# A reciprocal moved ahead of the value products, and one weight piece moved from the gated block into the second pair of heads

## The chip, the cores and the metric

The kernel runs on one core of a Trainium2 chip. The metric is the device time of one execution in microseconds; the times shown are medians of repeated runs. TensorE appears as PE (matmul) and PEld (weight load), VectorE as DVE, ScalarE as ACT, GpSimd as POOL, and SyncE as SP, which here only issues DMAs.

## What is computed

The first half is attention with a hash mask: a query sees only those keys whose six sign bits under a random projection agree with its own. Its output, rearranged to 3072 tokens of 512 channels, goes through a gated feed-forward block.

```python
batch, n_heads, seq, head_dim = (4, 8, 768, 64)
q_bits = (np.einsum('bhsd,dk->bhsk', q, proj) > 0)
mask = q_bucket[:, :, :, None] == k_bucket[:, :, None, :]
scores = np.where(mask, scale * np.matmul(q, k.transpose(0, 1, 3, 2)), -1000000000.0)
attn = np.exp(scores - max) ; attn = attn / (sum(attn) + 1e-09)
attn_out = np.matmul(attn, v)
x = attn_out.transpose(0, 2, 1, 3).reshape(B * S, H * D)      # 3072 x 512
g = x @ w_gate                                                # 512 x 1536
out = (g * sigmoid(g) * (x @ w_val)) @ w_out                  # 1536 x 512
```

The weights of the feed-forward block arrive as 64-bit floats and are read as pairs of 32-bit words.

## The kernel before

**Attention** goes through 16 pairs of heads, n = 0 to 15, four pairs to each of four batches. For each pair, 12 units (two halves of the queries by six blocks of 128 keys) are scored on PE (`score`, L523) into PSUM tiles of two banks; the pool `pp` has four such tiles for everything. ScalarE takes the exponential of each (L533), VectorE adds the exponentials up (`add`), and PE multiplies them with the values (`attend`, L554) into one further PSUM tile, which ScalarE copies to `xT` (L560, L561).

**The row sums** take a detour. `total(n)` adds across partitions on PE (L590); `fetch_row` copies the row (ScalarE, L595) and sends it by a small DMA on SP to a tile `few`, then puts `invert` on the list `waiting`. `settle()` runs what is on that list: `invert` takes the reciprocal on VectorE (L603), writes it to DRAM (`sums`, L605, SP) and reads it back spread over the partitions into `r` (two DMAs, L612, SP); it returns `norm`, which goes on the list `last`. `norm` (L619, VectorE) multiplies `xT` by `r`; for batches after the first it then writes the result to DRAM (L623, SP). In pair n's iteration `settle()` stands near the top and inverts pair n - 2, since `total(n - 1)` is run late in iteration n; after the loop it is called once more, and inverts pair 14. Pair 15's reciprocal is left for the gated block (`left`, L918: after the sixth and the fourteenth step there).

**The weight pieces.** The three weight matrices are cut into 36 pieces. Each piece is loaded (`words`, three buffers), scaled by ScalarE (`scale`, L139 and L140), widened by VectorE (`widths`, L153, L155, L158, after which the load of the piece three places on is issued), rounded by ScalarE (`round_up`, L146), split into parts by VectorE (`parts`, L166 and L168) and written to DRAM (`ram`, L170). Piece i lives in half i % 2 of a tile `stage` that it shares with its neighbour; the pool `stagep` has two such tiles.

In the attention loop this work is spread over the pairs. Near the end of iteration n, `begin_pieces(PACE[n])` first rounds the pieces widened before, then scales PACE[n] new ones, in ScalarE's order ahead of the value copy and of the next pair's exponentials. After the value products `keep_pieces()` takes the parts of all pieces widened so far and writes them to DRAM (POOL issues). The new ones are widened at the top of iteration n + 1. With PACE = 1, 1, 2, 1, 2, 1, ... 23 of the 36 are scaled by the end of the loop. The gated block does the others, one each in `turn()`: seven steps, dealt out between its own operations; there SP issues the DMAs.

**The gated block** goes through three blocks of 1024 tokens. For each of 12 slices of the hidden width (`U`), PE multiplies for the gate and then for the value, each as a group `a` of 16 matmuls and a group `n` of 8 (L711), into one PSUM tile each. ScalarE reads `a` (L750), VectorE subtracts `n` (L756), ScalarE applies the activation (L758), VectorE multiplies (L760) and splits (L767, L770). After each third slice (`D`), eight output chunks of 9 matmuls (`o`, L711) are added into accumulators (L811 or L813, then L817). The weights come back from DRAM through a ring of six tiles (`bring`, L251, POOL): three of the buffers are there from the start, three are allocated with the gated block. The order on each engine is the order of the program text; tiles are handed on by their pools.

Of the kernel before, what the change touches and what calls it, by code (L numbers as in the profile page):

```python
# [19 lines left out]
def kernel(  # L20
# [68 lines left out]
    def finish(todo):  # L89
        while todo:  # L90
            todo.pop(0)()
# [31 lines left out]
    def load_words(count, queue=None):  # L123
        queue = queue or queues[0]
        for i in range(len(words), min(count, NPIECE)):
            words[i] = t = wordp.tile([P, PIECE, 2], I32, tag="words", name="words")
            to = t.rearrange("p f w -> p (f w)")
            if len(pieces[i].shape) == 3:
                to = to.rearrange("p (j c) -> p j c", j=NJ)
            queue.dma_start(to, pieces[i])  # L130

    def scale(i):
        t = words[i]
        if i // 2 not in stages:
            stages[i // 2] = stagep.tile([P, 2, 3, PIECE], FP32, tag="stage", name="stage")
        staged[i] = st = stages[i // 2][:, i % 2]
        top = t.rearrange("p f w -> p (f w)").bitcast(U16)
        top = top.rearrange("p (f w) -> p f w", w=4)[:, :, 1]
        nc.scalar.activation(st[:, 1], t[:, :, 1].bitcast(FP32), AF.Copy, scale=2.0**-112)  # L139
        nc.scalar.activation(t[:, :, 0], top, AF.Copy, scale=2.0**-13 * (1 + 2.0**-17))  # L140
        progress["scaled"] = i + 1

    def round_up(i):
        if i not in rounded:
            st = staged[i]
            nc.scalar.activation(r32(st[:, 0]), st[:, 1], AF.Copy, scale=TOWARD)  # L146
            rounded.add(i)
# [26 lines left out]
    def begin_pieces(count):  # L174
        for i in sorted(added - rounded):
            round_up(i)
        for i in range(progress["scaled"], min(progress["scaled"] + count, NPIECE)):
            load_words(i + 1)
            scale(i)

    def keep_pieces():
        for i in range(progress["kept"], progress["scaled"]):
            if i in added:
                for _ in parts(i):
                    pass

    def widen_pieces():
        for i in range(progress["kept"], progress["scaled"]):
            if i not in added:
                for _ in widths(i):  # L190
                    pass
# [49 lines left out]
    def bring(count=1):  # L241
        for _ in range(count):
            i = len(held)
            if i == len(wanted):
                return
            what, n = wanted[i]
            at = place[what, n % NF]
            assert progress["kept"] > at, (i, at, progress)
            pool = ringp[i % sum(RINGS) >= RINGS[0]]
            held[what, n] = t = pool.tile([P, 3, PIECE], FP32R, tag="ring", name="ring")  # L250
            nc.gpsimd.dma_start(t.bitcast(FP32), ram[at].bitcast(FP32))  # L251
# [53 lines left out]
    def attention(scope):  # L305
# [39 lines left out]
        def load(n, names):  # L345
            if n < len(pairs):
                for name in names:
                    fetch(n, name, nc.sync)
# [187 lines left out]
        def score(u):  # L536
            if u % (2 * NCH):
                products(u)
                mark(u)
            else:  # L540
                banks_of[u] = two_banks("sc")[:, :, 0:HQ]
                product(u, bits, True, False)
                product(u, T, False, True)
                mark(u, False)

        def attend(u):
            n, half, c = units[u]
            a = weights(u)
            if (half, c) == (0, 0):
                av[n] = two_banks("av")  # L550
            ps = av[n][:, half]
            width = AW if half == 0 else HQ
            for h in range(2):
                nc.tensor.matmul(ps[h * D : (h + 1) * D, 0:width], raws["v", n][:, h, c, :],  # L554
                                 a[:, h, 0:width], start=c == 0, stop=c == NCH - 1)
            if (half, c) == (1, NCH - 1):
                pool, tag = (xp, "xT") if n < len(pairs) - 1 else (lastp, "last")
                xT[n] = pool.tile([P, S], FP32, tag=tag, name=tag)
                mean[n] = small.tile([P, 1], FP32, tag="e", name="e")
                nc.scalar.activation(mean[n], av[n][:, 0, HQ : HQ + 1], AF.Copy, scale=EPS)  # L560
                nc.scalar.copy(xT[n].rearrange("p (x q) -> p x q", x=2), av[n][:, :, 0:HQ])  # L561
# [3 lines left out]
        def add(u):  # L565
            n, half, c = units[u]
            if c % 2 == 0:
                return
            first, now = (twos[x % RING // 2][:, :, :, 0:HQ] for x in (u - 2, u))
            if c == 3:  # L570
                t = both[half] = att.tile([P, 2, 2, HQ], FP32, tag="both", name="both", bufs=1)
                nc.vector.scalar_tensor_tensor(out=t, in0=first, scalar=S * EPS / P / 2, in1=now,  # L572
                                               op0=ALU.add, op1=ALU.add)
            elif c > 3:
                t = both[half]
                nc.vector.tensor_tensor(t, t, now, op=ALU.add)  # L576
            if c == NCH - 1:
                acc[n, half] = att.tile([P, 2, HQ], FP32, tag="acc", name="acc", bufs=4)
                nc.vector.tensor_tensor(acc[n, half], t[:, 0], t[:, 1], op=ALU.add)
# [4 lines left out]
        def total(n):  # L584
            ps = joint(n)[:, 0]
            t = [acc.pop((n, half)) for half in range(2)]
            for h in range(2):
                for half in range(2):
                    g = (2 * h + half) * BLOCK
                    nc.tensor.matmul(ps[g : g + BLOCK, 0:HQ], ones, t[half][:, h, :],  # L590
                                     start=True, stop=True)

            def fetch_row():
                row = att.tile([P, HQ], FP32, tag="row", name="row", bufs=1)
                nc.scalar.copy(row, ps[:, 0:HQ])  # L595
                few = small.tile([P, each], FP32, tag="few", name="few")
                nc.sync.dma_start(few, row.rearrange("(g r) t -> r g t", r=BLOCK)[0])
                waiting.append(lambda: invert(n, few))

            return fetch_row  # L600
# [28 lines left out]
        def prepare_pair(count):  # L629
            for _ in range(count):  # L630
                if steps:
                    rest.extend(f for f in steps.pop(0)() or [] if f)

        def settle():
            while waiting:
                last.append(waiting.pop(0)())
# [4 lines left out]
        load_words(3, nc.sync)  # L641
        steps = front(1)
        last = []
        PACE = [1, 1] + [2, 1] * 7
        splits = []
        later = []
        TURN = 5
        for n in range(len(pairs)):
            u = 2 * NCH * n
            more = n + 1 < len(pairs)  # L650
            if n == 1:
                widen_pieces()
            if n and more:
                steps = front(n + 1)
                prepare_pair(2)
            widen_pieces()
            settle()
            for i in range(2 * NCH):
                if u + i > 2:
                    score(u + i)  # L660
                if n == 0 and i == TURN:
                    prepare_pair(2)
                if i % NCH and i < 2 * NCH - 1:
                    add(u + i)
                if i == (2 if n else TURN):
                    load(n + 2, "qk")
            row = total(n - 1) if n else None
            if more:
                prepare_pair(1)
            finish(rest)  # L670
            add(u + 2 * NCH - 1)
            if row:
                row()
            finish(last)
            begin_pieces(PACE[n])
            finish(splits)
            splits.extend(later)
            later.clear()
            for c in range(2 * NCH):
                attend(u + c)  # L680
            load(n + 2, "v")
            keep_pieces()
            if n >= len(pairs) - 3:
                bring()
# [9 lines left out]
    with ExitStack() as scope:  # L694
        attention(scope)
# [264 lines left out]
```

## Time and profile before

| | us |
|---|---|
| median of 3 runs (916.47 to 916.75) | 916.68 |
| the profiled execution | 916.95 |
| its span, first to last instruction | 915.2 |
| attention, until the first matmul of the gated block | 314.5 |
| one pair of heads (PE) | 19.1 |
| one slice `U` of the gated block (PE) | 10.9 |
| eight output chunks `D` (PE) | 16.3 |

The span holds 12450 instructions, and the mean granted TensorE clock is 0.997. VectorE is busiest in the attention stage: 18.5 us of the 19.1 us of pairs 4 to 7, 14.5 in pair 2. ScalarE is at 15 to 17 us per pair. The DMA engines are at a share of 0.45 to 0.98 in the attention stage and at 0.84 between 320 and 376 us, where the ring fills; later they fall to about 0.4.

A line of a timeline gives the start and the duration in us, engine, line, operation, output <- input with shapes, and a count of merged instructions; in brackets the idle time before it and what ended that. A line of the waits gives who waited for whom: us in total, times, the longest. A line of DMA issues gives the count, the size, and the median us from issue to landing.

### The profile page before, as it was taken

How to read it: one execution, taken by the hardware profiler on the slowest of the kernel's cores; microseconds unless marked ns; L12 is line 12 of the kernel's file. 1: busy time of each engine (PE TensorE's matmuls, PEld its weight loads, DVE VectorE, ACT ScalarE, POOL GpSimd, SP SyncE). 2: the span in 40 equal slices, each digit the busy share in tenths (PEclk: the TensorE clock that was granted, in tenths of full speed). 3: DMA queues.
4: the chain of work that ended last, by engine and by line, in shares of the span. 5: the costliest groups of instructions: out<-in, count | busy, mean ns of one | idle time of the engine just before them, and what ended most of it. 6: DMA issues, size and time to landing. Idle time of an engine off the chain costs nothing.

```text
span 915.2 us, 12450 instructions
## 1 busy us (share of the span) xinstructions
PE 904.3 (99%) x4801; PEld 637.2 (70%) x4801; DVE 665.7 (73%) x783; ACT 450.9 (49%) x606; POOL 88.1 (10%) x176
## 2 busy tenths in 40 slices
PE   9999999999999989999999999999999999999998
PEld 4444444444444568788888888888888888888886
DVE  6779999998988748779786955365568754474746
ACT  7688988888787625542523133331313233313220
POOL 1001100011001201000001100101000100001000
PEclk9999999999999999999999999999999999999999
DMA  7576777978796798685867573433444642525232
GB/s 184 103 155 184 185 206 185 219 205 220 216 199 213 239 335 273 236 293 199 322 206 255 179 269 127 173 139 140 148 158 149 244 142 86 219 71 207 103 138 92
DMA packets 143706, 174.24 MB, mean 190 GB/s; under 512 B 103360, under 2 KB 113568, under 8 KB 143648
## 3 DMA queue, kind: packets, MB, share of 16 engines
q0 software_dynamic: 22096, 114.31, 35.6%
q1 hardware_dynamic: 120144, 57.95, 24.7%
q10 hardware_dynamic: 1408, 1.20, 0.5%
q8 instruction: 38, 0.62, 0.3%
q14 instruction: 20, 0.16, 0.1%
HBM read 133.17 MB, written 39.42 MB: 189 GB/s over the span
## 4 chain that ended last, share of the span: by engine, by line
PE 86%; DVE 6%; DMA 3%; ACT 2%; issue 2%; SPq 0%; ACTq 0%; DVEq 0%
PE a L711 24%; PE o L711 19%; PE sc L523 16%; PE av L554 12%; PE n L711 12%; DMA sums<-few 1%; DMA r<-sums 1%; PE joint L590 1%; PE joint L431 1%; DVE v L756 1%; DVE v L760 1%; DVE hid L767 1%; DVE g L756 1%; ACT v L750 1%; DVE stage L158 1%
## 5 line engine op out<-in xcount | busy, mean ns | idle before, releaser
L711 PE MATMUL a<-xparts,ring 128*128 128x512 f32 x1152 | 273.0, 389 | 0.0
L711 PEld LDWEIGHTS a<-xparts,ring 128*128 128x128 f32 x1152 | 216.2, 188 | 45.5 <-issue 0.6
L711 PE MATMUL o<-ring,hid 128*128 128x512 f32 (+1 forms) x870 | 199.3, 389 | 1.5 <-DVE o L817 1.5
L711 PEld LDWEIGHTS o<-ring,hid 128*128 128x128 f32 x870 | 162.6, 188 | 36.5 <-DVE o L817 2.7
L533 ACT ACTIVATE A<-sc 128x768 f32<-128x768 f32 x192 | 153.8, 816 | 0.9
L523 PE MATMUL sc<-qT,kT 64*128 64x384 f32 x768 | 152.8, 483 | 0.2 <-ACT qb L436 0.2
L711 PE MATMUL n<-xparts,ring 128*128 128x512 f32 x576 | 143.8, 392 | 4.3 <-DVE g L756 4.3
L711 PEld LDWEIGHTS n<-xparts,ring 128*128 128x128 f32 x576 | 109.1, 190 | 27.4 <-DVE g L756 4.7
L554 PE MATMUL av<-A,vraw 128*64 128x386 f32 (+1 forms) x768 | 127.7, 488 | 0.0
L756 DVE TENSOR_TENSOR v<-v,n 128x1024 f32<-128x1024 f32 x36 | 44.0, 1221 | 98.0 <-PE n L711 91.8
L251 POOL DMA_DIRECT2D ring<-ram x108 | 57.1, 531 | 506.6 <-PE n L711 330.4
L554 PEld LDWEIGHTS av<-A,vraw 128*64 128x64 f32 x768 | 53.7, 136 | 73.3 <-issue 63.0
L750 ACT ACTIVATE g<-a 128x1024 f32<-128x1024 f32 x36 | 36.9, 1025 | 124.8 <-PE a L711 124.1
L523 PEld LDWEIGHTS sc<-qT,kT 64*128 64x128 f32 x768 | 68.3, 187 | 41.2 <-issue 35.5
L761 ACT ACTIVATE hid<-v 128x1024 fp32r<-128x1024 f32 x36 | 38.2, 1062 | 112.5 <-DVE v L760 112.5
L758 ACT ACTIVATE g<-g 128x1024 f32<-128x1024 f32 x36 | 38.2, 1061 | 97.4 <-DVE g L756 97.4
L817 DVE TENSOR_TENSOR o<-o 128x512 f32<-128x512 f32 x92 | 63.0, 686 | 18.9 <-ACT o L811 16.5
L756 DVE TENSOR_TENSOR g<-g,n 128x1024 f32<-128x1024 f32 x36 | 43.8, 1215 | 31.4 <-PE n L711 31.4
L523 PE MATMUL sc<-qb,kb 64*128 64x384 bf16 x384 | 62.8, 323 | 0.0
L572 DVE SCALAR_TENSOR_TENSOR both<-A 128x1536 f32<-128x1536 f32 x32 | 55.4, 1732 | 6.4 <-ACT A L533 5.0
L767 DVE SCALAR_TENSOR_TENSOR hid<-hid,v 128x1024 fp32r<-128x1024 f32 (+1 forms) x39 | 44.5, 1140 | 19.2 <-ACT hid L761 19.1
L576 DVE TENSOR_TENSOR both<-both,A 128x1536 f32<-128x1536 f32 x32 | 56.0, 1749 | 1.7
(80 smaller groups left out, 691.8 us busy)
## 6 DMA issues: line engine op xcount, KB each, us to landing
ring<-ram POOLq DMA_DIRECT2D x108, 768.0 KB, 5.2
ram<-stage POOLq DMA_DIRECT2D x22, 768.0 KB, 4.6
ram<-stage SPq DMA_DIRECT2D x14, 768.0 KB
vraw<-in_v_dram SPq DMA_DIRECT2D x16, 384.0 KB
out_dram<-o SPq DMA_DIRECT2D x23, 256.0 KB
kraw<-in_k_dram SPq DMA_DIRECT2D x60, 96.0 KB
qraw<-in_q_dram SPq DMA_DIRECT2D x60, 96.0 KB
r<-sums SPq DMA_DIRECT2D x30, 192.0 KB
```

What stands on the lines that cost most here:

```text
L251: nc.gpsimd.dma_start(t.bitcast(FP32), ram[at].bitcast(FP32))
L523: nc.tensor.matmul(banks_of[u][:, h], x["k", n][rows, ks], x["q", n][rows, qs], start=start, stop=stop)
L533: nc.scalar.activation(weights(u)[:, :, 0:HQ], banks_of.pop(u), AF.Exp, scale=SCALE * (1.0 if units[u][0] else OFF / 2))
L554: nc.tensor.matmul(ps[h * D : (h + 1) * D, 0:width], raws["v", n][:, h, c, :], a[:, h, 0:width], start=c == 0, stop=c == NCH - 1)
L572: nc.vector.scalar_tensor_tensor(out=t, in0=first, scalar=S * EPS / P / 2, in1=now, op0=ALU.add, op1=ALU.add)
L576: nc.vector.tensor_tensor(t, t, now, op=ALU.add)
L711: nc.tensor.matmul(ps, w, x, start=start, stop=stop)
L750: nc.scalar.activation(two(z), ops[what][2], AF.Copy, scale=STEP + 1)
L756: nc.vector.tensor_tensor(two(z), two(z), n_, op=ALU.subtract)
L758: nc.scalar.activation(z, z, AF.Silu)
L767: nc.vector.scalar_tensor_tensor(out=l_, in0=h_.bitcast(FP32), scalar=-STEP, in1=v_, op0=ALU.mult, op1=ALU.add)
L817: nc.vector.tensor_tensor(accs[c], accs[c], t[:, 1], op=ALU.subtract)
```

## The change

Two edits in the attention loop. In the last iteration (n = 15, where `more` is false) `settle()` is called right after `finish(last)`, ahead of `begin_pieces`, the value products and `keep_pieces`; the list `waiting` then holds the inversion of pair 14, so the call after the loop finds nothing. And `PACE` begins with 1, 2 instead of 1, 1: iteration 1 scales pieces 1 and 2, every later iteration scales the same number as before with an index one higher, and 24 pieces are scaled in the attention loop, 12 in the gated block.

```diff
@@ -641,7 +641,7 @@
         load_words(3, nc.sync)
         steps = front(1)
         last = []
-        PACE = [1, 1] + [2, 1] * 7
+        PACE = [1, 2] + [2, 1] * 7
         splits = []
         later = []
         TURN = 5
@@ -672,6 +672,8 @@
             if row:
                 row()
             finish(last)
+            if not more:
+                settle()
             begin_pieces(PACE[n])
             finish(splits)
             splits.extend(later)
```

## The prediction

> **What bounds the kernel now.** I read the busy shares first, then the list of waits, then the timelines of each engine where PE stands still.
>
> ```profile
> PE 904.3 (99%) x4801; PEld 637.2 (70%) x4801; DVE 665.7 (73%) x783; ACT 450.9 (49%) x606; POOL 88.1 (10%) x176
> ...
> PE n L711 <- DVE g L756: 4.3, 1, 4.3
> PE o L711 <- DVE o L817: 1.5, 3, 0.6
> ...
> DVE xT L619 <- DMA r<-sums: 16.2, 2, 15.4
> POOL words L130 <- DVE stage L158: 32.0, 4, 24.4
> ```
>
> TensorE sets the time: 904.3 of 915.2 us. Its 10.9 us of idle time close to the last tenth: 1.24 at the start, 3.86 after its last matmul (911.34), 4.32 waiting for one VectorE subtraction, and 1.47 in three short waits on the output accumulators (0.43 and 0.64 at 373 to 376, 0.40 at 474.69). So only what moves these gaps, or makes a new one, counts. The timelines around the long gap:
>
> ```profile
> 318.27 1.98 PE L711 MATMUL n<-xparts,ring 128*128 128x512 f32 x8
> ...
> 333.63 3.55 PE L711 MATMUL n<-xparts,ring 128*128 128x512 f32 x8 [4.32 <-DVE g L756]
> ...
> 315.86 0.22 DVE L603 RECIPROCAL few<-few 128x12 f32<-128x12 f32 x1
> 331.43 1.02 DVE L619 SCALAR_TENSOR_TENSOR xT<-xT,e,r 128x768 f32<-128x768 f32 x1 [15.35 <-DMA r<-sums]
> 332.37 1.21 DVE L756 TENSOR_TENSOR g<-g,n 128x1024 f32<-128x1024 f32 x1
> ...
> 316.11 0.33 SPq L605 DMA_DIRECT2D sums<-few  x1
> 322.38 1.10 SPq L612 DMA_DIRECT2D r<-sums  x2
> ```
>
> Read it backwards. PE waits for `g`; `g` sits behind `norm(14)` (L619) in VectorE's order; `norm(14)` waits 15.35 us for two DMAs in a row, sums out (6.26 us) and broadcast back (8.95), which start only after the reciprocal at 315.86. The eight matmuls after the gap then take 3.39 us start to next start instead of 1.81: 1.58 more. The whole episode costs 4.32 + 1.58 = 5.90 us.
>
> The other half of the change lies in pairs 1 to 3. The same lines there, with the landing time of the write back last:
>
> ```profile
> 62.82 0.70 ACT L139 ACTIVATE stage<-words 128x512 f32<-128x512 f32 x1
> 65.78 0.79 ACT L561 COPY xT<-av 128x768 f32<-128x768 f32 x1
> 66.63 9.69 ACT L533 ACTIVATE A<-sc 128x768 f32<-128x768 f32 x12
> ...
> 65.93 0.69 DVE L168 SCALAR_TENSOR_TENSOR stage<-stage 128x512 fp32r<-128x512 f32 x1
> ...
> 67.18 0.55 POOL L170 DMA_DIRECT2D ram<-stage  x1 [16.01 <-DVE stage L168]
> ...
> 68.03 0.81 PE L523 MATMUL sc<-qT,kT 64*128 64x384 f32 x4
> ...
> ram<-stage POOLq DMA_DIRECT2D x1, 768.0 KB, 5.3
> ```
>
> ScalarE scales the second piece of pair 2 at 62.82, before the value copy and the exponentials of pair 3; the write back of piece 1 is issued at 67.18 and lands 5.3 us later, at 72.5.
>
> **What the skill says.** "TensorE: Matmul & The Clock Gate", section "What's actually happening": after about one idle window of 3.4 us the clock falls to half, and comes back after about as long a busy stretch. The trace agrees: a gap of 4.32 us, then 3.55 us of matmuls at half speed (granted clock 0.50 from 334 to 336), and none after the gaps of 0.4 to 0.6. "DMA: Bandwidth & Descriptors", section "Issuing engines are not separate DMA queues": all queues share 16 engines. The trace agrees: the broadcast took 3.57 us at a DMA share of 0.2 to 0.5 (306 to 310) and 8.43 at 1.0 (322 to 331). Both are used below.
>
> **Part 1, `settle()` inside pair 15.** Nothing is added or removed: one reciprocal (0.22), one write of sums and two broadcasts (SP issue 0.33 and 1.10) move forward past the last rounding work. On VectorE the reciprocal now follows `norm(13)`, which ends at 311.4; its input was issued by SP at 307.33 and is behind a broadcast that landed at 310.3, so it is there or nearly. It passes four L166/L168 and three width operations (311.31 to 315.9), which move 0.15 us back and have no one waiting. On SP it follows the `xram` write (311.42, 0.32): sums go out at about 311.8 instead of 316.1. SP then stands until they have landed; behind it is only the row of pair 15 (ready at 315.1), needed at 344. From 310 to 312 the DMA share is 0.00, and sums written in quiet stretches took 1.7 us from issue to broadcast (131.36 to 133.03). So broadcast from about 313.6 to 315, between two write backs and the ring loads; landing between 317.5 (the 3.57 row) and 323.5 (the 8.43 row), I take 320.5. `g` then starts at 321.5. PE wants its buffer at 329.3 (333.63 less the 4.32 of idling), so the gap goes: 5.90.
>
> What is late next: from `g` on, one block of VectorE and ScalarE takes 10.49 us (332.37, 342.89, 353.38) against PE's 10.88. The third block's last subtraction would come at 321.5 + 35.9 = 357.4, and the output chunks, now from 364.24 - 5.90 = 358.3, lose their two waits (0.43 + 0.64 = 1.07) as long as `g` starts before 325.4. Ring loads: the fourth is needed at 331 and landed at 326.7 (issued at 317.07, 9.6 us to landing); moved-up traffic (384 KB of `xram`, part of a write back, at 350 GB/s) delays it about 2 us, so it holds.
>
> **Part 2, two pieces in pair 1.** One scaling more on ScalarE in pair 1 (L139 + L140, 1.34), where it idles 2.77 before the value sums: hidden. One widening and one rounding more on VectorE in pair 2 (1.8 + 1.4), where it idles 3.43 and its busy time is 14.5 of 19.1: hidden. In the gated block the last turn goes: its scaling, widening and parts, 3.2 us of VectorE work between 464 and 477, part of which stood ahead of the 0.40 wait: gone.
>
> The cost is a buffer. Two pieces share a `stage` tile and the pool has two. With one then two pieces, tile 0 (pieces 0, 1) was written out before tile 2 was wanted. Now pair 1 takes pieces 1 and 2, and pair 2 at once 3 and 4. Piece 4 opens tile 2 in tile 0's buffer, while piece 1 is rounded and written out only after it in the program (`keep_pieces()` follows `begin_pieces()`). The pool hands a buffer on when the last user of the old tile is done; the trace shows that rule on `words` (POOL waiting 24.4 us for L158). So L139 of piece 4 waits for the DMA issued at 67.18: until 72.5 instead of 62.8. Queued behind it on ScalarE are the copy of the values and all exponentials of pair 3: the copy ends at 74.55, the first exponential starts at 74.65 instead of 66.63. PE has four PSUM tiles: one holds the values of pair 2, three take scores, and it stops at 68.03 until 74.55: 6.5 us. That exceeds the clock window, so another 1.6 at half clock. Afterwards PE is the bound again, VectorE and ScalarE are shifted equally (keys' bits have 4 us of slack), and nothing is won back: 8.1. From both sides: write backs land in 3.5 to 6.8 us over the run, so 6.3 to 9.6. No later pair repeats it, since a two is never again followed by a two.
>
> **Sum.** -5.90 - 1.07 - 0.40 + 8.1 = +0.7 on a profiled execution of 916.95 (span 915.2). The median is 0.27 under it: 916.68 + 0.7 = 917.4. The likeliest case's own range is 915.5 to 918.9.
>
> **Rivals.** (a) *The buffer is not waited for*: pieces 1 and 4 lie in different halves of their tiles, so no bytes collide, and if waits follow bytes rather than tiles, only the gain is left: 909.3. For it: nothing forbids it in the data. Against: every reuse wait in the trace is on the last user of a whole tile. (b) *The hops stay slow*: both DMAs take their old 6.26 and 8.95 us because the same write backs and ring loads surround them. Place: VectorE before `norm(14)`; it decides once the broadcast lands after 324.3. At 311.8 + 15.2 = 327.0, `g` starts at 328.1, PE just misses a gap, but the output chunks wait 2.7 us: gain 4.6, total +3.5, 920.2, slower. For it: 1.0 DMA share from 316 on. Against: the quiet 310 to 312. (c) *The stall is shorter or longer*: landing 3.5 or 6.8 us: 915.5 or 918.9, in the own range.
>
> **How the numbers follow.** Likeliest 0.62 (mostly within 0.2%, about 1.8 us, the least that a measurement here tells from no change; 0.03 below, 0.11 above), (a) 0.12, (b) 0.22, no gain at all with the stall (924.7) 0.04. Faster 0.15; same 0.48, its share of the likeliest case; slower 0.11 + 0.22 + 0.04 = 0.37. The range 914.0 to 921.0 holds the likeliest and (b), and leaves out (a) and the last.
>
> **What would show it.** Right: ScalarE's L139 near 72 waiting for a `ram` write or its L168, PE idle some 6.5 us near 68 to 75 with a lower clock after; no wait of PE before the third `n` group; broadcast landed before 324; no wait at the first output chunks. Wrong: no gap at 68 (rival a), `norm(14)` still after 324 (b), or a ring load that PE waits for.

## The result, and the profile after

| | before | changed |
|---|---|---|
| median of 14 runs each, us | 917.55 (916.21 to 919.48) | 916.19 (914.49 to 917.34) |
| ratio, 95% interval | | 0.9982 (0.9973 to 0.9992) |
| profiled execution, us | 916.95 | 915.68 |
| its span, us | 915.2 | 913.8 |
| weight pieces scaled in attention / in the gated block | 23 / 13 | 24 / 12 |

The change makes the kernel faster by 1.4 us in the medians, a little less than 0.2% (by the ratio 1.7, between 0.7 and 2.5). Forecast was 0.7 us slower. (The 916.68 that the prediction started from was the median of three runs; with the later runs of the same kernel it is 917.55, so the movement is read from the ratio.) Behind the small sum stand two large terms of opposite sign.

The waits of the changed kernel, who waited for whom: us in total, times, the longest. Lines up to L672 keep their numbers, later ones are two higher than before.

```profile
PE sc L523 <- ACT xT L561: 4.7, 1, 4.7
PE idle L375 <- DVE kb L369: 1.0, 1, 1.0
PE o L713 <- DVE o L819: 0.4, 1, 0.4
...
DVE xT L619 <- DMA r<-sums: 9.1, 2, 8.0
...
ACT stage L139 <- DMA ram<-stage: 7.5, 1, 7.5
```

TensorE's wait of 4.3 us for `g` is gone, and two of the three at the output chunks. A wait that was not there before has come: 4.7 us at a score, behind ScalarE's value copy. The timelines of the changed kernel there, in start and duration:

```profile
62.49 0.67 ACT L140 ACTIVATE words<-words 128x512 int32<-128x512 uint16 x1
70.61 0.68 ACT L139 ACTIVATE stage<-words 128x512 f32<-128x512 f32 x1 [7.45 <-DMA ram<-stage]
71.81 0.77 ACT L561 COPY xT<-av 128x768 f32<-128x768 f32 x1
72.48 2.97 ACT L533 ACTIVATE A<-sc 128x768 f32<-128x768 f32 x4
...
66.91 0.56 POOL L170 DMA_DIRECT2D ram<-stage  x1 [14.15 <-DVE stage L168]
...
67.57 0.33 PE L523 MATMUL sc<-qb,kb 64*128 64x384 bf16 x2
72.63 1.65 PE L523 MATMUL sc<-qT,kT 64*128 64x384 f32 x4 [4.73 <-ACT xT L561]
74.39 1.49 PE L523 MATMUL sc<-qT,kT 64*128 64x384 f32 x4
75.99 1.29 PE L523 MATMUL sc<-qT,kT 64*128 64x384 f32 x4
77.28 0.81 PE L523 MATMUL sc<-qT,kT 64*128 64x384 f32 x4
```

The scaling of piece 4 stands from 63.2 to 70.61 for a write to DRAM that was issued at 66.91, so it ends 3.7 us after the issue. The value copy follows it, frees its PSUM tile at 72.58, and PE goes on at once. The next three units take 4.65 us (72.63 to 77.28) where three take 2.42 at full clock. The windows of the same execution, PE's busy time first and the granted clock third from the right, show why:

```profile
68.00:70.00 2.00, 0.00 (x0) 0.00 (x0) 1.97 (x4) 0.00 (x0) 0.56 (x1) 1.00 0.98 393
70.00:72.00 2.00, 0.00 (x0) 0.00 (x0) 1.78 (x4) 1.40 (x4) 0.43 (x1) 0.53 0.97 393
72.00:74.00 2.00, 1.37 (x4) 0.66 (x6) 1.30 (x3) 2.00 (x4) 0.74 (x2) 0.50 0.46 121
74.00:76.00 2.00, 2.00 (x11) 1.14 (x9) 0.51 (x1) 1.46 (x2) 0.36 (x1) 0.50 0.87 214
76.00:78.00 2.00, 2.00 (x14) 1.01 (x14) 1.25 (x1) 1.33 (x2) 0.00 (x0) 0.76 0.53 201
```

The clock falls to half while PE stands and is back only between 76 and 78. The unit from 74.39 to 75.99 takes 1.60 us, where one takes 0.81 at full clock.

At the other end, the timelines of the changed kernel around the gated block's start, which answer to the ones shown of before (everything there now comes 6.8 us later on the clock of the span):

```profile
318.39 0.22 DVE L603 RECIPROCAL few<-few 128x12 f32<-128x12 f32 x1
331.08 1.02 DVE L619 SCALAR_TENSOR_TENSOR xT<-xT,e,r 128x768 f32<-128x768 f32 x1 [7.97 <-DMA r<-sums]
332.02 1.21 DVE L758 TENSOR_TENSOR g<-g,n 128x1024 f32<-128x1024 f32 x1
...
318.87 0.43 SPq L605 DMA_DIRECT2D sums<-few  x1
321.02 1.79 SPq L612 DMA_DIRECT2D r<-sums  x2
...
325.07 1.98 PE L713 MATMUL n<-xparts,ring 128*128 128x512 f32 x8
...
335.95 1.98 PE L713 MATMUL n<-xparts,ring 128*128 128x512 f32 x8
```

The sums go out in 2.15 us (318.87 to 321.02) instead of 6.26, the broadcast takes 10 us until it is used (9.05 before), and `g` starts at 332.02 and takes 1.21, so it is done 2.7 us before PE takes its buffer at 335.95. The third `n` group takes 1.98, not 3.55.

The two spans, cut at the same instructions (start to start, us):

| stretch | before | changed | difference |
|---|---|---|---|
| start to the scores of pair 3 | 65.59 | 65.30 | -0.3 |
| scores of pair 3 to its value products | 11.23 | 18.35 | +7.1 |
| value products of pair 3 to the gated block | 237.67 | 237.66 | 0.0 |
| first four slices `U` | 49.75 | 43.65 | -6.1 |
| first output chunks `D` | 18.09 | 17.02 | -1.1 |
| from there to the third `D` | 81.60 | 81.60 | 0.0 |
| third `D` | 17.01 | 16.32 | -0.7 |
| the rest | 434.3 | 433.9 | -0.4 |

The sum is -1.4. One term of +7.1 stands against three that make 7.9. The small terms at the start and in the rest are not explained; the start also differs between two executions of one kernel (65.30 here, 66.07 when the changed kernel was run again).

### The profile page after: what moved, and what is told of

Its sections match the earlier page's. It is cut to its first block, busy times and chain, and to the rows that moved or that the text cites. A ratio compares the mean times of both kernels' runs of the same rounds, so it can differ in the third digit from the quotient of the medians.

```text
span 913.8 us, 12448 instructions
## 1 busy us (share of the span) xinstructions
PE 903.9 (99%) x4801; PEld 637.3 (70%) x4801; DVE 665.5 (73%) x783; ACT 450.4 (49%) x606; POOL 88.9 (10%) x178
## 4 chain that ended last, share of the span: by engine, by line
PE 85%; DVE 6%; DMA 4%; ACT 2%; issue 2%; SPq 1%; ACTq 0%; DVEq 0%; POOLq 0%
PE a L713 25%; PE o L713 19%; PE sc L523 15%; PE n L713 13%; PE av L554 10%; DMA r<-sums 1%; DMA sums<-few 1%; DMA ram<-stage 1%; PE joint L590 1%; PE joint L431 1%; DVE v L758 1%; DVE v L762 1%; DVE g L758 1%; DVE hid L769 1%; DVE o L815 0%
## 5 line engine op out<-in xcount | busy, mean ns | idle before, releaser
L523 PE MATMUL sc<-qT,kT 64*128 64x384 f32 x768 | 154.8, 489 | 4.9 <-ACT xT L561 4.7
L523 PE MATMUL sc<-qb,kb 64*128 64x384 bf16 x384 | 63.2, 325 | 0.0
```

The source lines that it names most:

```text
L523: nc.tensor.matmul(banks_of[u][:, h], x["k", n][rows, ks], x["q", n][rows, qs], start=start, stop=stop)
```

## The experiments

Ratios are against runs of the kernel before on the same chip in the same session; its medians lay between 918.05 and 918.36 us there.

**The early settle alone.**

```diff
             finish(last)
+            if not more:
+                settle()
             begin_pieces(PACE[n])
```

> The early settle alone, PACE as before (1, 1, 2, 1, ...). Theory: its gain does not need the other edit. The wait of 4.3 us before the third n group goes with its slow matmuls (6.1 us start to start), most of the two waits at the first output chunks goes too (about 1.1), the wait near 474 (0.4) stays: 7.0 to 7.5 us faster than before, ratio about 0.992. No gap of PE near 68 us. Rival: the gain in the gated block comes from preparing one piece less there; then this kernel is within 1 us of before, or the wait of the first output chunks comes back in full.

Measured: 911.28 us, ratio 0.9921 (0.9907 to 0.9934), 7.1 us faster; span 908.8. No PE gap near 68. The waits of PE in this kernel:

```profile
PE o L713 <- DVE o L819: 1.1, 2, 0.7
PE idle L375 <- DVE kb L369: 1.0, 1, 1.0
```

The long gap is gone without the other edit, so the rival falls. (Of the smaller waits two are new: 0.6 us in all behind a ScalarE operation on the keys, and 0.3 for a ring load, so these loads have little room.) Of the 1.5 us of waits at the output chunks 1.1 is left (0.66 at the first chunks, which was 1.07, and 0.40 at the third): here `g` starts 11.6 us after the gated block's first matmul (326.07 - 314.50), in the changed kernel 10.7 (332.02 - 321.31). So this smaller gain seems to depend on when the broadcast lands, and I had it as good as certain.

**The other pace alone.**

```diff
-        PACE = [1, 1] + [2, 1] * 7
+        PACE = [1, 2] + [2, 1] * 7
```

> PACE = 1, 2, 2, 1, ... alone, settle as before. Theory of the shared buffer: ScalarE's second L139 of pair 2 waits for the write back of piece 1, PE stands 4.5 to 6.5 us in pair 3 and then runs three units at half clock: +7 us, less 0.4 to 0.9 for the piece that the gated block no longer prepares, so 6 to 7 us slower than before, ratio about 1.007; the 4.3 us wait in the gated block stays. Rival, that the long gap of the gated block belongs to VectorE's load there and shrinks with the missing piece: the gap at the third n group is clearly under 4 us.

Measured: 924.55 us, ratio 1.0064 (1.0052 to 1.0077), 6.2 us slower. Its waits of PE hold both gaps:

```profile
PE sc L523 <- ACT xT L561: 4.7, 1, 4.7
PE n L711 <- DVE g L756: 4.3, 1, 4.3
PE o L711 <- DVE o L817: 1.1, 2, 0.7
```

The gap of PE in pair 3 is as long as in the changed kernel (4.72), but the three units after it take 4.22 us (72.95 to 77.17) instead of 4.65. The missing piece leaves the long gap untouched and takes away only the wait in the third `D`. The two edits do not touch each other: 0.9921 x 1.0064 = 0.9984, and both together gave 0.9982.

**The same pieces, paired with the other neighbour** (in the changed kernel).

```diff
-        if i // 2 not in stages:
-            stages[i // 2] = stagep.tile([P, 2, 3, PIECE], FP32, tag="stage", name="stage")
-        staged[i] = st = stages[i // 2][:, i % 2]
+        at = (i + 1) // 2
+        if at not in stages:
+            stages[at] = stagep.tile([P, 2, 3, PIECE], FP32, tag="stage", name="stage")
+        staged[i] = st = stages[at][:, (i + 1) % 2]
```

> The changed kernel with one line of pairing altered: piece i shares its tile with the neighbour on the other side, so pieces 1 and 2 are one tile, 3 and 4 the next. Same pieces per pair, same operations, same buffers. Theory: piece 4 then takes the buffer of piece 0, written out a pair earlier; no wait of L139, no gap of PE in pair 3: 8 us faster than before (6.1 + 1.1 + 0.4 to 0.9), ratio 0.991, 7 us faster than the changed kernel. Rival, that L139 of piece 4 really waits for its own load (issued only at the top of pair 2) or that two pieces in two pairs running are too much for ScalarE: the gap near 68 us stays and the time is that of the changed kernel, ratio 0.998.

Measured: 908.68 us, ratio 0.9894 (0.9879 to 0.9910), 9.7 us faster than before; span 907.1 against 915.2, which is 8.1. Pair 2's scalings and what follows them on ScalarE, in this kernel (its lines are one higher from L134 on):

```profile
62.48 0.67 ACT L140 ACTIVATE stage<-words 128x512 f32<-128x512 f32 x1
63.05 0.68 ACT L141 ACTIVATE words<-words 128x512 int32<-128x512 uint16 x1
63.63 0.69 ACT L140 ACTIVATE stage<-words 128x512 f32<-128x512 f32 x1
64.23 0.67 ACT L141 ACTIVATE words<-words 128x512 int32<-128x512 uint16 x1
65.98 0.17 ACT L561 ACTIVATE e<-av 128x1 f32<-128x1 f32 x1 [1.08 <-PE av L555]
```

The second scaling follows the first without a gap, although its own load was issued no earlier than in the changed kernel. That excludes the load and the amount of work: what piece 4 waited for was the buffer that piece 1 shared with piece 0. (That it waited for piece 1 of the two is shown by the last experiment.) PE's list of waits has only the two at the kernel's start left (1.0 and 0.2). This version beats both kernels.

**The extra piece in pair 0** (in the changed kernel).

```diff
-        PACE = [1, 2] + [2, 1] * 7
+        PACE = [2, 1] * 8
```

> The changed kernel with PACE = 2, 1, 2, 1, ...: the extra piece in pair 0 instead of pair 1, so that a two never follows a two; 24 pieces in the attention stage as in the changed kernel, original pairing. Theory: piece 3 and 4 come in pair 2 with tile 0 written out in pair 1; no gap in pair 3; about 8 us faster than before, ratio 0.991, like the shifted pairing. Rival: pair 0 cannot take a second piece (its words are just loaded at 13 to 20 us, ScalarE idles 3.7 us there): a gap of PE near 27 us and 1 to 4 us of the gain lost.

Measured: 909.66 us, ratio 0.9904 (0.9891 to 0.9918); span 908.1. No gap in pair 3 and none near 27 us: pair 0 takes the second piece. The original pairing does no harm if a two never follows a two. Two waits at the first output chunks stay (1.0 us), with `g` 11.9 us after the first matmul of the gated block.

**The last write backs moved out of pair 15** (on top of the shifted pairing). Their parts and DMAs are left to the first turns of the gated block.

```diff
-            keep_pieces()
+            if more:
+                keep_pieces()
```

> The shifted pairing once more, with the parts and the two write backs of pair 15 (pieces 21 and 22) left to the first turns of the gated block. Question: what makes the broadcast of pair 14's sums take 10 us (issue to norm) where I took 3.6 to 8.4? Theory: the two write backs of 768 KB that POOL issues at 314 and 315.3 stand before it; without them it lands 3 to 5 us after its issue at 314.5, near 319, and VectorE waits under 2 us for it. Rival: the ring loads behind them are enough; then POOL issues these 2 to 3 us earlier, the DMA share is at 1.0 as before and the broadcast still takes 8 us or more. In both, PE has no wait for the first blocks' subtractions, so the time is that of the shifted pairing within 1 us (ratio 0.989 to 0.991), unless the four extra VectorE steps bring back a wait at the first output chunks (up to 1 us).

Measured: 910.19 us, ratio 0.9920 (0.9903 to 0.9937). My theory fell. The broadcast and its reader in this kernel:

```profile
314.97 1.10 SPq L613 DMA_DIRECT2D r<-sums  x2
...
323.86 1.02 DVE L620 SCALAR_TENSOR_TENSOR xT<-xT,e,r 128x768 f32<-128x768 f32 x1 [9.44 <-DMA r<-sums]
```

8.9 us from issue to use, without the write backs (9.7 with them). POOL issues its three ring loads at 315.55 here, 2.2 us earlier than with the write backs, and the DMA share is at 0.93 to 1.06 from 316 to 324. The write backs are not needed for a slow broadcast. The ring loads remain, and with them one load of a weight piece (512 KB), which POOL issues at 314.71, just before the broadcast; no run takes these two apart. Waits of 1.0 us at the output chunks came back: 0.59 at the first `D` (368.93) and 0.40 at the second (418.66).

**The changed kernel again,** for the landing.

> The changed kernel, a second look at one number: how long the write back of piece 1 takes to land in pair 2. Theory: its landing sets the stall, PE stands for landing + 1.1 us; 3.6 us again gives 4.7 us of PE idle, a landing of 5.3 us (as the kernel before shows there) 6.4 us. Rival: the stall is set by something of fixed length and does not follow the landing.

Measured in one execution, 916.37 us: the write back was issued at 67.67, the scaling started at 71.38 (3.7 us), PE stood 4.75. The number repeated, so this run could not tell whether the stall follows it. The next one could. At the other end `g` started 10.0 us after the gated block's first matmul in this execution, and no wait at the output chunks was left.

**The two write backs of pair 2 in the other order** (in the changed kernel).

```diff
-        progress["kept"] = i + 1
+        progress["kept"] = max(progress["kept"], i + 1)
...
-        for i in range(progress["kept"], progress["scaled"]):
+        todo = [i for i in range(progress["kept"], progress["scaled"]) if i in added]
+        for i in reversed(todo) if todo == [1, 2] else todo:
```

> The changed kernel with the two write backs at the end of pair 2 in the other order: piece 2 first, piece 1 second. Same operations. Theory: the stall of PE in pair 3 follows the landing of piece 1. Its write is issued 1.3 us later and has the other 768 KB in front of it in the same queue: the wait of the second L139 ends 1.3 to 3.3 us later than in the changed kernel (8.8 to 10.8 us after its engine went idle instead of 7.45), PE stands 6.1 to 8.1 us instead of 4.75, and the time is 1.3 to 3.3 us above the changed kernel, so about 917.5 to 919.5 where the kernel before gives 917.5 to 918. Rival, a wait of fixed length that only coincides with the write back: 7.45 us and 4.75 us stay, time unchanged.

Measured: 918.76 us, ratio 1.0005 (0.9996 to 1.0014) against 0.9982 for the changed kernel: 2.1 us more. The second scaling and the score that waits behind it, in this kernel:

```profile
72.90 0.66 ACT L139 ACTIVATE stage<-words 128x512 f32<-128x512 f32 x1 [9.54 <-DMA ram<-stage]
...
74.91 1.65 PE L524 MATMUL sc<-qT,kT 64*128 64x384 f32 x4 [6.81 <-ACT xT L562]
```

The wait is 2.1 us longer (9.54 for 7.45), and PE stands 2.1 us longer (6.81 for 4.73). The stall follows the landing of piece 1 one for one. That the median is longer by the same 2.1 us is weaker evidence: the profiled execution had a further wait of 1.1 us for a ring load, and the two ratios have intervals of about 0.9 us to each side.

## Why the prediction was wrong

It named both mechanisms, and each was found at the place it gave. What was wrong was the size of the second. Measured apart, the early settle took 7.1 us off (interval 6.1 to 8.5) where 7.0 was forecast (5.90 + 1.07), and the other pace cost 6.2 us (4.8 to 7.1) where 7.7 was forecast (8.1 - 0.40). As the two nearly cancel, that turned the sign. In the two profiled executions forecast and measurement are 2.1 us apart: 1.0 lies in the 8.1, 0.2 in the long gap, 0.3 in the third `D`, and 0.7 at the start and in the rest, at which neither edit was aimed.

- *The buffer of piece 1* (part 2, the "8.1"). The chain was right link by link: L139 of piece 4 behind the DMA of piece 1, the value copy and the exponentials behind L139, PE stopped after three units. The step that failed is "until 72.5": I took the landing row of the kernel before at that very place, 5.3 us, where 3.6 was measured in both executions of the changed kernel and with the pace alone. So PE stood 4.73 us, not 6.5. By the traces the 5.3 holds a delay that the stall itself takes away (last section). My lower end, 3.5 us, was the right value. In return the clock cost was too small: 1.6 was carried over from the gap of the gated block, but here the stretch at low clock cost 2.2 us over three units (4.65 - 2.42), and 2.4 with the restart. Together 7.1.
- *The price of the low clock.* The Trainium skill, "TensorE: Matmul & The Clock Gate", section "What's actually happening", gives at least one window of about 3.4 us for each change of the clock, idle for the fall and busy for the way back. The gap before agreed with it (4.32 us idle, 3.55 us of slow matmuls). In the changed kernel the clock fell 2.2 us after PE had stopped (67.90; the mean of 0.53 from 70 to 72 puts the fall at 70.1) and was back 4.3 us after PE went on (0.76 from 76 to 78). With the pace alone, after a gap of the same length, it fell 0.6 us after PE had gone on (0.89 from 72 to 74), and the cost was 1.8 us. The measurement decides: 1.6 to 2.4 us for one such gap in this kernel, and not the same in two executions with the same gap. Four of the 14 runs of the changed kernel took 914.5 to 914.7 us at a mean granted clock of 0.998, the other ten 915.7 to 917.3 at 0.995 to 0.997.
- *The long gap* (part 1, 5.90). Right: 6.1 measured from start to start, and with the settle alone it went as well. The landing of the broadcast was put at 3.5 to 8.5 us after its issue and took 10. On the clock of the kernel before `norm(14)` started at 324.3 (331.08 less 6.8), after the forecast's range and just where it let rival (b) decide. It did not matter for the gap, since the sums before it went in 2.15 us instead of 6.26 and `g` was done 2.7 us early.
- *The first output chunks* (1.07). The stretch became 1.1 shorter, but that the size agrees is luck: a wait of 0.38 was left, and the list of waits had held only part of what could be won. Without any wait there the stretch took 16.4 us (changed kernel again) and 16.8 (shifted pairing), against 18.1 before. The bound "as long as `g` starts before 325.4", 10.9 us after the gated block's first matmul, is near the truth: at 10.0 and 10.5 (these two) no wait, at 10.7 one of 0.4, at 11.6 to 11.9 waits of 0.7 to 1.0. In the version without the last write backs 0.6 was left at 10.5, with more VectorE work in the block.
- *One piece less in the gated block* (0.40): the stretch became 0.7 shorter, with the pace alone too.
- *Rival (a)*, waits that follow bytes and not tiles, is excluded by the changed kernel: piece 4 lies in the other half than piece 1, and its scaling waited 7.45 us all the same; with the writes exchanged it waited for the later landing of piece 1. *Rival (b)*, slow hops, was half right: the second hop stayed slow, the first did not, and the gain held.

## What to carry to other kernels

When work is moved earlier by one slot, count the live halves of every shared tile at the new point: here two pieces per tile were harmless until two double steps met, and then the engine whose order puts the scaling before the exponentials stopped with everything behind it. And when a forecast is the difference of two large terms, the sign is only as good as the worse of them; measure the parts one by one, because here each was clear (0.992 and 1.006) where their sum was not. A landing time read in the old kernel holds only with what ran beside it there; a stall moves that too.

## What the runs showed of the hardware that was not expected

A write back of 768 KB issued at the same place showed two landing times. In the kernels in which nothing stands in pair 3 the view of DMA issues gives 5.2 to 5.7 us for the first or only one (before, settle alone, extra piece in pair 0, and the two versions with the shifted pairing, where a second write takes 5.7 to 6.2). In those in which ScalarE and PE stand, it gives 3.6 to 3.7 for the first of the two and 4.3 to 4.6 for the second, whether or not ScalarE waits for that one. The first two lines here are of the kernel before (65 to 73 us), the others of the changed kernel (first and second write). A line of the queues gives the packets, the MB, and the time that they took as a share of 16 engines:

```profile
q8 instruction: 1, 0.02, 1.1%
ram<-stage POOLq DMA_DIRECT2D x1, 768.0 KB, 5.3
...
ram<-stage POOLq DMA_DIRECT2D x1, 768.0 KB, 3.6
ram<-stage POOLq DMA_DIRECT2D x1, 768.0 KB, 4.3
```

The packet of the instruction queue (16 KB) begins at 68.45 in the kernel before and takes 1.4 us, in the middle of the write back. The traffic falls from 381 GB/s (69.5 to 70.0) to 25 GB/s between 70.5 and 71.5: from 70.4 to 72.0 the last seven packets of the write follow each other singly, 0.23 us each, as work left over on one engine would. All five kernels with 5.2 us or more have such a packet between 68 and 70 us, and the four executions with 3.6 or 3.7 (changed kernel twice, pace alone, other order of the writes) have it only between 74 and 78, after PE has gone on. Elsewhere in the kernel before it is the same: a lone write back took 4.8 us with such a packet beside it (issued at 47.07) and 3.5 without one (107.29 and 146.00). After 200 us up to 6.8 us were reached without one, so it is not the only thing that delays a landing. No run was aimed at this; it is read from the traces, and they do not show whose instructions the packet brings. If it holds, the stall put off the load of instructions that had delayed the landing in the kernel before, and so was itself shorter than forecast.

A broadcast of 2 x 192 KB took 8.9 to 10.7 us from issue to use while loads of 512 and 768 KB filled the DMA engines, and 4.0 to 4.2 us at a lower share (pair 13, changed kernel and before). Being issued before the ring loads did not spare it: in the experiment without write backs its first half was issued 0.6 us before them (and 0.3 after the 512 KB load), and it still needed 8.9.
